# A planned transformer kernel: teaching the planner that GpSimd and VectorE exclude each other at an SBUF port

## The chip, the cores and the metric

One core of a Trainium2 chip. Time is device time in microseconds (us) for one execution of the whole program. Five engines work side by side, each on its own queue of instructions, in that queue's order: TensorE (PE in the profile, its weight loads PEld), ScalarE (ACT), VectorE (DVE), GpSimd (POOL) and SyncE (SP, which issues the DMAs). They meet at semaphores only.

## What is computed

Two layers, each an attention block and an MLP block, on 2,048 tokens of width 512. The weights of both layers are the same. There are 32 heads of width 16, and the MLP is 1,792 wide. Cut to its core, the reference is:

```python
def attention(x):                       # x is normalised
    q, k, v = split(x @ wqkv)           # 32 heads of 16
    p = softmax(q @ k.T * 16 ** -0.5)   # 2048 x 2048 for each head
    return (p @ v) @ wo
def mlp(x):
    return gelu(x @ w1 + b1) @ w2 + b2
for _ in range(2):
    x = x + attention(layernorm(x))
    x = x + mlp(layernorm(x))
```

Data are bfloat16. With heads this narrow the exponentials of the softmax are the bulk of the work: 2 layers x 32 heads x 2048 x 2048 of them.

## The kernel before

**Tiling.** Scores are computed transposed, keys on the 128 partitions and queries along the row. One *cell* is one matmul of TensorE (L1137): 128 keys by 512 columns, that is one bank of PSUM. There are 4,096 cells. A cell then goes one of two ways:
- to ScalarE: L1466 takes the exponential of two or three cells in one instruction (1,024 or 1,536 columns) and writes bfloat16 tiles `pt`. The two slots for this are PSUM banks 0 to 2 and 3 and 4.
- to VectorE, for some rows of keys (`KD`): L1283 (`dfirst`) turns the scores in PSUM into 16-bit integers that are close to the bits of an exponential, into the tile `du` (`dh` for a single one, `kt` where it lies in borrowed space). L1344 and L1346 (`dchain`) then add constants to make three shifted copies. These two work on 16-bit integers from SBUF to SBUF.

The probabilities are multiplied with the values by matmuls of L1527 into PSUM bank 5, 17 rows for each head: 16 of output and one of the row's sum. `norm` finishes a pass: it may add a stored partial sum (L739), transposes into the one buffer `xt` (L741, L743), takes the reciprocal of the sums into `rc` (L746), multiplies by it into `ott` (L754, on GpSimd or on VectorE; two buffers) and transposes into `otn` (L759). From there the output projection `wo` (matmuls of L512, addition to the residual at L785), the layer norm (L581 to L602, its last multiplication `xln` mostly on GpSimd, its power of -0.5 at L588 on GpSimd), and the MLP (`hpair`, `gelu` at L893, `ytile` with the addition at L925) run for 512 tokens at a time, in the shadow of the following tokens' attention. GpSimd also pads the queries of a pass (`qp`, L1085) and scales values for the integer path (`vc`, L1068).

**What sets the order.** No queue's order is written by hand. While the program is built, on the host, `_Sched` runs every part as a thread that yields operations with a price in microseconds, and keeps a clock for each engine. Again and again `run` takes, for each engine, the operations whose inputs are known; among those that could start at once it picks the one of lowest priority number, else the one that is ready first; and of all engines it places the one with the earliest start. The order of placing becomes the engine's queue, and the semaphores that are needed are put in. Prices are fixed; for example:

```python
yield _Op("dve", 0.08 + 0.14 * n, lambda e: e.tensor_scalar(U[:, 1, 0:n, :], U[:, 0, 0:n, :], SHIFT, None, op0=ALU.add),
eng, cost = ("dve", 0.4) if quick else ("pool", 0.72)
```

An operation's output counts as ready at the end of its price plus a small `LATENCY`. The planner also decides during the run: `attach` and `swap` send a cell to VectorE when a bank and a `du` buffer are free in the plan, and `fill` puts dummy matmuls (L1125) into TensorE's planned idle time[...]; `free` chooses their bank. What the chip does differently from the plan can't be made good later: a queue waits at whatever instruction stands first.

Buffers that a plan must not give out twice are *pools*: `("acq", name)` takes the next free one, `("take", ...)` a certain one, `("rel", ...)` gives it back.

**The end.** When the last exponentials are done, ScalarE does the gelu of the last but one group of 256 tokens (two instructions), while the last group (tiles 14 and 15) still needs `norm`, `wo`, its layer norm, and its whole MLP. Tiles 12 and 13 have only their second MLP product left, in pieces of eight matmuls and a last one of twelve.

Of the kernel before, what the change touches and what calls it, by code (L numbers as in the profile page):

```python
# [31 lines left out]
DU = 9  # L32
# [48 lines left out]
class _Prog:  # L81
# [4 lines left out]
    def __init__(self, sems):  # L86
        self.sems = sems
        self.cnt = {k: 0 for k in sems}
        self.prog = {e: [] for e in self.ENGS}
        self.K = {e: {} for e in self.ENGS}  # L90
        self.ev_k = {}
        self.lastw = {}
        self.reads = {}
# [108 lines left out]
        self.done = False  # L202


LATENCY = {"pe": 0.20, "act": 0.10, "dve": 0.10, "pool": 0.15, "sp": 0.1}


class _Sched:
# [5 lines left out]
    def __init__(self, P):  # L214
        self.P = P
        self.clock = {e: 0.0 for e in P.ENGS}
        self.end = {}
        self.pools = {}
        self.tokens = {}
        self.threads = []  # L220
        self.nseq = 0
        self.mode = "F"
        self.ops = []
        self.stream = []
        self.filler, self.free, self.fills = None, None, set()

    def pool(self, name, slots):
        self.pools[name] = list(slots)
# [66 lines left out]
    def _prio(self, op):  # L295
        return op.prio() if callable(op.prio) else op.prio

    def landed(self, keys):
        return max(self.end.get(self.P.lastw[k], 0.0) if k in self.P.lastw else 1e9 for k in keys)

# [11 lines left out]
    def fill(self, start, nxt):  # L312
        while self.filler and self.mode:
# [17 lines left out]
            self.clock["pe"] = now + into + MM + cold  # L331
            self.end[ev] = self.clock["pe"] + LATENCY["pe"]

    def run(self):
        while True:
            moved = True
            while moved:
                moved = False
                for th in list(self.threads):
                    if self._advance(th):  # L340
                        moved = True
            self.threads = [t for t in self.threads if not t.done]
            best = {}
            for th in self.threads:
                if th.op is None:
                    continue
                e = th.op.eng
                rdy = self._ready(th.op)
                if rdy is None:
                    continue  # L350
                best.setdefault(e, []).append((th, rdy))
            if not best:
                if self.threads:
                    raise RuntimeError("stuck: %r" % [(t.prio, t.block) for t in self.threads])
                return
            pick = None
            for e, cand in best.items():
                now = self.clock[e]
                nowc = [c for c in cand if c[1] <= now]
                if nowc:  # L360
                    ch = min(nowc, key=lambda c: (self._prio(c[0].op), c[0].seq))
                else:
                    ch = min(cand, key=lambda c: (c[1], self._prio(c[0].op), c[0].seq))
                start = max(now, ch[1])
                stop = start + self._cost(ch[0].op)
                for c in cand:
                    if c[0].op.slack is not None and c is not ch and c[1] + c[0].op.slack < stop:
                        ch = c
                        start = max(now, ch[1])
                        break  # L370
                if pick is None or start < pick[0]:
                    pick = (start, e, ch[0])
            start, e, th = pick
            op = th.op
            th.op = None
            if op.late is not None:
                op.late(op, start)
            if e == "pe":
                mode = self.mode
                self.fill(start, op)  # L380
                if mode != self.mode:
                    start = max(self.clock["pe"], start - SW * (op.mode != self.mode) + SW * (op.mode != mode))
            ev = self.P.group(e, op.fns, op.reads, op.writes, op.sem, op.by)
            cost = self._cost(op)
            if e == "pe":
                self.mode = op.mode
                self.note(start + cost - op.cost, start + cost, op)
            self.ops.append((e, start, cost, op.writes[0] if op.writes else ""))
            self.clock[e] = start + cost
            self.end[ev] = start + cost + op.tail + LATENCY[e]  # L390

# [110 lines left out]
class _Plan:  # L502
# [215 lines left out]
    def norm(self, l, seg, g, b, part, final):  # L718

        T = self.T  # L720
        pv = self.bank(b)
        key = "B.%d" % b
        qc, q0, w = seg
        if qc == 0:
            pt, pk = T["PART"][l][:, g, :], "PART.%d.%d" % (l, g)
            over = ["V0.%d" % k for k in range(self.NT)] + ["V01"] if l else []
        else:
            pt, pk = T["PART1"][:, g, :], "PART1.%d" % g
            over = ["K0.%d.%d" % (g // 2, c) for c in range(self.NQ)]
        prev = self.before(l, seg)  # L730
        if final and prev:
            yield ("need", ("ofree",) + prev)
        if not final:
            yield _Op("dve", DV, lambda e: e.tensor_copy(pt, pv), reads=[key], writes=[pk] + over)
            yield ("rel", "pv", b)
            return
        xt = T["XT"]
        if part:
            yield _Op("dve", DV, lambda e: e.tensor_tensor(out=pt, in0=pt, in1=pv, op=ALU.add), reads=[key, pk], writes=[pk])  # L739
            yield ("rel", "pv", b)  # L740
            yield _Op("dve", 0.7, lambda e: e.transpose(xt[:, :], pt), reads=[pk], writes=["XT"])  # L741
        else:
            yield _Op("dve", 0.7, lambda e: e.transpose(xt[:, :], pv), reads=[key], writes=["XT"])  # L743
            yield ("rel", "pv", b)
        x3 = xt[:, :].rearrange("p (k c) -> p k c", c=32)
        yield _Op("dve", 0.23, lambda e: e.reciprocal(T["RC"][:, :].rearrange("p (k o) -> p k o", o=1), x3[:, :, 16:17]),  # L746
                  reads=["XT"], writes=["RC"])
        gb, ts = self.heads(seg, g)
        o = gb % 2
        pool = g < 6 and seg[2] == 512  # L750
        nb = w // 32
        for i, t in enumerate(ts):
            o3 = T["OTT"][:, o, 0:w].rearrange("p (k c) -> p k c", c=32)[:, :, 16 * t:16 * t + 16]
            yield _Op(*(("pool", 0.1 + 0.55 * w / 512) if pool else ("dve", 0.1 + 0.31 * w / 512)), lambda e, i=i, o3=o3: e.tensor_tensor(  # L754
                out=o3, in0=x3[:, i * nb:i * nb + nb, 0:16],
                in1=T["RC"][:, i * nb:i * nb + nb, None].to_broadcast([128, nb, 16]), op=ALU.mult),
                reads=["XT", "RC"], writes=["OTT.%d.%d" % (o, t)])
        if ts[-1] == 1:
            yield _Op("dve", 0.05 + 0.65 * w / 512, lambda e: e.transpose(T["OTN"][:, gb, q0:q0 + w], T["OTT"][:, o, 0:w]),  # L759
                      reads=["OTT.%d.0" % o, "OTT.%d.1" % o],  # L760
                      writes=["OTN.%d.%d" % (gb, t % 4) for t in self.tiles(seg)])
            yield ("give", ("otn", l, seg, gb))

    def heads(self, seg, g):
# [325 lines left out]
    def free(self, now, ahead):  # L1090
        P = self.P
        best = (None, 1e9)
        src = self.source()
        for b in (6, 7, 0, 1, 2, 3, 4, 5) if src else ():
            k = "B.%d" % b
            if k in ahead or b in self.hold or k in P.lastw and not P.reads.get(k) and P.lastw[k] not in self.s.fills:
                continue
            t = max([0.0] + [self.s.end.get(ev, 0.0) + FOLD for ev in P.deps(src, [k]) if ev[0] != "pe"])
            if max(t, now) < max(best[1], now):
                best = (b, t)  # L1100
        k = "B.%d" % PVB
        if best[1] > now and self.pvopen and "VC.0.0" in P.lastw and k not in ahead:
            best = (PVB, 0.0)
        return best
# [65 lines left out]
    def take(self, c, free):  # L1170
        self.scored += 1
        self.left[c[0]] -= 1
        if self.left[c[0]] == 0:
            free.append(self.s.tokens[("qp", c[0])])
# [385 lines left out]
    def run(self):  # L1560
        s = self.s
        self.phase = {}
        s.pool("misc", MISC)
        s.pool("dbank", [])
        s.route = self.route
        s.pool("pv", [PVB])
        s.pool("s", range(len(SLOTS)))
# [54 lines left out]
```

The softmax here doesn't subtract the row's maximum and nothing guards it: scores larger than these inputs give would overflow.

## Time and profile before

| | |
|---|---|
| time, median of 3 | 1588.41 us (1587.63 to 1589.98) |
| profiled span | 1587.3 us |
| ScalarE busy | 1547.1 us |
| TensorE busy | 1424.2 us |
| VectorE busy | 1352.0 us |
| GpSimd busy | 200.5 us, in 250 instructions |
| cells to ScalarE / to VectorE | 3,207 / 889 |

A row of the profile's groups reads: line, engine, operation, output and inputs by the program's names, shape, count; then busy time, mean duration of one in ns; then the engine's idle time just before these instructions and what ended most of it. In a timeline each row has its start, its length, the engine, the line and the instruction; where several like ones follow each other they are one row with a count.

### The profile page before, as it was taken

The numbers are of one execution on the slowest core, as the hardware profiler recorded it, in microseconds if no ns is written. First come the engines' busy times: TensorE is split into PE (matmuls) and PEld (weight loads), VectorE is DVE, ScalarE is ACT, GpSimd is POOL, SyncE is SP. The second block draws the span as 40 slices with busy tenths as digits, with TensorE's granted clock in tenths as the row PEclk, the third lists the DMA queues.
The fourth block names the chain that finished last, engine by engine and source line by source line (L and its number), as shares of the span: only waits on it lengthen the run. The fifth ranks groups of instructions, "written<-read, shape, count | busy, mean of one in ns | idle before, by whom it ended". The sixth has DMA issues, their size and how long they took to land.

```text
span 1587.3 us, 42896 instructions
## 1 busy us (share of the span) xinstructions
PE 1424.2 (90%) x18701; PEld 444.6 (28%) x18701; DVE 1352.0 (85%) x2564; ACT 1547.1 (97%) x1393; POOL 200.5 (13%) x250
## 2 busy tenths in 40 slices
PE   8998888899999898988989998888998889898988
PEld 3222222222222222222222222222222222333344
DVE  5689999888898889978788789899878988998984
ACT  7999999999999999999999999999999999999996
POOL 5200012001100201002120020122001000010000
PEclk9999999999999999999999999999999999999999
DMA  5100001241114311143111510001251105312520
GB/s 140 22 2 1 2 14 41 77 132 46 27 45 130 85 41 28 42 140 74 36 28 48 172 44 28 1 2 33 67 167 43 28 15 151 103 36 87 155 82 29
DMA packets 141767, 96.88 MB, mean 61 GB/s; under 512 B 36877, under 2 KB 141582, under 8 KB 141582
## 3 DMA queue, kind: packets, MB, share of 16 engines
q1 hardware_dynamic: 141582, 94.14, 21.2%
q8 instruction: 149, 2.44, 0.6%
q14 instruction: 36, 0.29, 0.1%
HBM read 84.41 MB, written 2.10 MB: 55 GB/s over the span
## 4 chain that ended last, share of the span: by engine, by line
ACT 67%; PE 29%; DVE 2%; POOL 1%; issue 1%; DMA 0%; ACTq 0%; POOLq 0%
ACT pt L1466 60%; PE ps L512 11%; PE ps L1137 9%; PE ps L1527 8%; ACT g L893 3%; ACT v L1466 2%; ACT kt L1466 1%; ACT q L1466 1%; DVE du L1283 1%; ACT L893 1%; ACT L1466 0%; DMA xf<-xln 0%; PE ps L1125 0%; POOL xln L602 0%; POOL rstd L588 0%
## 5 line engine op out<-in xcount | busy, mean ns | idle before, releaser
L1466 ACT ACTIVATE pt<-ps 128x1536 bf16<-128x1536 f32 (+2 forms) x1261 | 1384.2, 1246 | 15.2 <-PE ps L1137 10.3
L1137 PE MATMUL ps<-qp,kt 32*128 32x512 bf16 x4096 | 538.0, 385 | 140.8 <-ACT pt L1466 106.7
L1283 DVE TENSOR_SCALAR du<-ps 128x512 uint16<-128x512 f32 x711 | 479.7, 685 | 97.5 <-PE ps L1137 89.6
L1527 PE MATMUL ps<-pt,v 128*17 128x512 bf16 (+1 forms) x3368 | 433.8, 359 | 2.3 <-ACT pt L1466 0.8
L1527 PE MATMUL ps<-du,vc 128*17 128x512 bf16 (+1 forms) x2394 | 333.8, 358 | 2.7 <-DVE du L1346 1.4
L1137 PEld LDWEIGHTS ps<-qp,kt 32*128 32x128 bf16 x4096 | 140.6, 91 | 685.9 <-ACT pt L1466 304.2
L1346 DVE TENSOR_SCALAR du<-du 128x2048 uint16<-128x2048 uint16 x361 | 246.3, 687 | 2.5
L1085 POOL TENSOR_SCALAR qp<-q,mask 128x512 bf16<-128x512 bf16 (+1 forms) x91 | 66.3, 728 | 1013.8 <-PE ps L1137 1005.1
L512 PE MATMUL ps<-xf,wr 128*32 128x512 bf16 (+1 forms) x2400 | 170.8, 368 | 1.7 <-DMA xf<-xln 1.1
L1527 PE MATMUL ps<-du,v 128*17 128x512 bf16 (+1 forms) x798 | 154.7, 360 | 1.7 <-DVE xt L743 0.9
L1344 DVE TENSOR_SCALAR du<-du 128x1024 uint16<-128x1024 uint16 x361 | 150.5, 428 | 2.0
L1527 PEld LDWEIGHTS ps<-pt,v 128*17 128x17 bf16 x3368 | 111.8, 89 | 113.0 <-issue 72.9
L512 PE MATMUL ps<-wr,g 128*32 128x512 bf16 x1600 | 123.8, 384 | 5.5 <-ACT g L893 5.0
L1527 PEld LDWEIGHTS ps<-du,vc 128*17 128x17 bf16 x2394 | 92.5, 89 | 62.7 <-issue 27.5
L872 DVE TENSOR_SCALAR g<-ps,hb1t 128x512 bf16<-128x512 f32 (+1 forms) x112 | 79.8, 713 | 13.8 <-PE ps L512 12.9
L1527 PE MATMUL ps<-dh,vc 128*17 128x512 bf16 (+1 forms) x321 | 90.6, 358 | 0.0
L1283 DVE TENSOR_SCALAR dh<-ps 128x512 uint16<-128x512 f32 x96 | 65.8, 685 | 11.5 <-PE ps L1137 10.8
L1283 DVE TENSOR_SCALAR kt<-ps 128x512 uint16<-128x512 f32 x82 | 56.1, 684 | 20.7 <-PE ps L1137 19.9
L512 PEld LDWEIGHTS ps<-xf,wr 128*32 128x32 bf16 x2400 | 53.6, 95 | 61.5 <-issue 33.5
L602 POOL TENSOR_SCALAR xln<-x,rstd,nmr 128x512 bf16<-128x512 bf16 x58 | 58.2, 1008 | 33.3 <-DMA xf<-xln 23.2
L754 POOL TENSOR_TENSOR ott<-xt,rc 128x256 bf16<-128x256 f32 x42 | 29.5, 703 | 178.5 <-DVE rc L746 178.5
L1125 PE MATMUL ps<-vc 128*32 128x512 bf16 x476 | 50.9, 395 | 0.1
(93 smaller groups left out, 1185.2 us busy)
## 6 DMA issues: line engine op xcount, KB each, us to landing
wr<-in_B_w_dram SPq DMA_DIRECT2D x256, 256.0 KB, 2.9
wr<-in_A_wqkv_dram SPq DMA_DIRECT2D x24, 256.0 KB, 2.9
wr<-in_A_wo_dram SPq DMA_DIRECT2D x18, 256.0 KB, 2.9
out_dram<-x SPq DMA_DIRECT2D x16, 128.0 KB, 2.7
g<-in_A_wqkv_dram SPq DMA_DIRECT2D x3, 512.0 KB, 5.1
x<-in_A_x_dram SPq DMA_DIRECT2D x3, 512.0 KB, 8.0
q<-in_B_w_dram SPq DMA_DIRECT2D x3, 512.0 KB, 3.9
kt<-in_B_w_dram SPq DMA_DIRECT2D x4, 256.0 KB, 3.3
```

What stands on the lines that cost most here:

```text
L512: return [lambda e, a=a: e.matmul(out[32 * a:32 * a + 32, :], lhsT=lhsT[:, 32 * a:32 * a + 32], rhs=rhs, start=start, stop=stop, tile_posi ...
L602: yield _Op(eng, cost, lambda e: e.tensor_scalar(T["XLN"][:, x, :], T["X"][:, t, :], T["RSTD"][:, t:t + 1], T["NMR"][:, t:t + 1], op0=ALU. ...
L872: yield _Op("dve", 0.21 + n / 966, lambda e, fc=fc, pb=pb: e.tensor_scalar(T["G"][:, fc, q], pb, T["HB1T"][:, fc:fc + 1], None, op0=ALU.ad ...
L893: lambda e, g=g: e.activation(out=g, in_=g, func=ACT.Gelu_apprx_tanh), reads=gk, writes=gk, prio=2)
L1085: yield _Op("pool", 0.1 + 0.6 * w / 512, lambda e, s=s, q=q, i=i, t=t, w=w: e.tensor_scalar(T["QP"][:, s, w * i:w * i + w], q, T["MASK"][: ...
L1125: fns.append(lambda e, o=o, w=w, a=a, m=m: e.matmul(o, lhsT=w, rhs=rhs, start=start, stop=start, tile_position=(0, m * a)))
L1137: return (lambda e: e.matmul(o, lhsT=lhsT, rhs=rhs, start=True, stop=True, tile_position=(32 * a, 0)), ["K%d.%d.%d" % (l, gb, kt // 4), "Q ...
L1283: yield _Op("dve", 0.68, lambda e: e.tensor_scalar(u, self.bank(b), E_SCALE, E_BIAS, op0=ALU.mult, op1=ALU.add), reads=["B.%d" % b], write ...
L1344: yield _Op("dve", 0.08 + 0.14 * n, lambda e: e.tensor_scalar(U[:, 1, 0:n, :], U[:, 0, 0:n, :], SHIFT, None, op0=ALU.add), reads=key[0], w ...
L1346: yield _Op("dve", 0.08 + 0.28 * n, lambda e: e.tensor_scalar(U[:, 2:4, 0:n, :], U[:, 0:2, 0:n, :], 2 * SHIFT, None, op0=ALU.add), reads=k ...
L1466: yield _Op("act", 0.065 + 0.4267 * n, lambda e, src=src, dst=dst: e.activation(out=dst, in_=src, func=ACT.Exp, scale=0.25), reads=["B.%d" ...
L1527: op.fns.append(lambda e, o=o, lhsT=q[0][0][m], rhs=q[0][1][:, n * m:n * m + n], a=a, st=st, sp=sp: e.matmul(o, lhsT=lhsT, rhs=rhs, start= ...
```

## The change

The planner learns of one more resource. GpSimd's instructions (all but the power, whose output is `RSTD`) and those VectorE instructions that work from SBUF to SBUF in the integer path or write `XLN` are called *locking*. For each of the two engines the last few locking operations are kept with the stretch in which they hold the port: from 0.05 us after the planned start to 0.13 us before the planned end (`HOLD`). When a locking operation is looked at, `unlocked` moves its ready time behind such a stretch of the other engine; VectorE is let through while it follows closely on its own last locking operation. So another operation that is ready earlier may be placed first.

Three things go with it. Because operations may now be held back, `norm` takes `xt` and `ott` from pools, and gives them back when their last reader is placed. The start of `norm` waits for `xt` before it adds to or releases its PSUM bank. And `free` no longer offers bank 5 to the filler in its general list.

No instruction's work, no buffer and no price is changed. The diff, cut to its core:

```diff
+HOLD = (0.05, 0.13)
 LATENCY = {"pe": 0.20, "act": 0.10, "dve": 0.10, "pool": 0.15, "sp": 0.1}
...
+        self.locks = {"pool": [], "dve": []}
+        self.fast = (0.0, 0.0)
...
+    def locking(self, op):
+        w = op.writes[0] if op.writes else ""
+        if op.eng == "pool":
+            return not w.startswith("RSTD")
+        return op.eng == "dve" and (w.startswith("XLN") or w.startswith("DU") and w.split(".")[2] != "0")
+
+    def unlocked(self, op, rdy):
+        if op.eng not in self.locks or not self.locking(op):
+            return rdy
+        now = t = max(rdy, self.clock[op.eng])
+        for a, b in self.locks["pool" if op.eng == "dve" else "dve"]:
+            if a <= t < b and not (op.eng == "dve" and a >= self.fast[0] and t < self.fast[1] + 0.02):
+                t = b
+        return t if t > now else rdy
...
-                best.setdefault(e, []).append((th, rdy))
+                best.setdefault(e, []).append((th, self.unlocked(th.op, rdy)))
...
+            if self.locking(op):
+                self.fast = (start, start + cost) if e == "dve" else self.fast
+                self.locks[e] = self.locks[e][-3:] + [(start + HOLD[0], start + cost - HOLD[1])]
...
         xt = T["XT"]
+        gb, ts = self.heads(seg, g)
+        yield ("acq", "xt")
...
-        gb, ts = self.heads(seg, g)
         o = gb % 2
+        if ts[0] == 0:
+            yield ("take", ("ott", o))
...
+        yield ("rel", "xt", 0)
...
+            yield ("rel", "ott", o)
...
-        for b in (6, 7, 0, 1, 2, 3, 4, 5) if src else ():
+        for b in (6, 7, 0, 1, 2, 3, 4) if src else ():
...
+        s.pool("xt", [0])
+        s.pool("ott", [0, 1])
```

## The prediction, made before the changed kernel was run

> **What bounds the kernel now.** I read the page first: engine shares, then the chain that ended last, then the costliest groups.
>
> ```profile
> PE 1424.2 (90%) x18701; PEld 444.6 (28%) x18701; DVE 1352.0 (85%) x2564; ACT 1547.1 (97%) x1393; POOL 200.5 (13%) x250
> ...
> ACT 67%; PE 29%; DVE 2%; POOL 1%; issue 1%; DMA 0%; ACTq 0%; POOLq 0%
> ...
> L1466 ACT ACTIVATE pt<-ps 128x1536 bf16<-128x1536 f32 (+2 forms) x1261 | 1384.2, 1246 | 15.2 <-PE ps L1137 10.3
> ```
>
> ScalarE (ACT) is the bound: 97% busy, two thirds of the chain, nearly all of it the softmax exponentials of L1466. The other engines matter only when they make an exponential late. The 15.2 us of idle time in the row understates that. Two exponentials that don't have to wait overlap at their ends. From the start times in the trace, a 1,024-wide one is followed by the next after 0.904 us and a 1,536-wide one after 1.331 us (medians of those that nothing holds up). The program has 793 of the first, 540 of the second and one of 512. Their real start-to-start times add up to 759.1 + 723.3 us, against 793 x 0.904 + 540 x 1.331 = 1435.6 us. So about 47 us are lost between exponentials, and that is the whole pool from which a better plan can draw. 41.6 us of it lie in some 160 single delays of over 40 ns.
>
> Next, who is late. The waits, longest in total first, show TensorE's score matmuls (L1137) waiting for VectorE to empty a PSUM bank:
>
> ```profile
> PEld ps L1137 <- DVE du L1283: 89.6, 152, 1.6
> DVE du L1283 <- PE ps L1137: 89.6, 180, 3.1
> ```
>
> The second line warns that VectorE also waits for TensorE. By the last wait that ended before the late score, about 19 of the 41.6 us go to VectorE, 12 to the exponentials themselves (a bank that came free late) and 10 to other matmuls ahead in TensorE's queue.
>
> Then the disputed resource. First VectorE, then GpSimd (POOL), in order of time (start, duration, instruction):
>
> ```profile
> 250.96 0.42 DVE L1344 TENSOR_SCALAR du<-du 128x1024 uint16<-128x1024 uint16 x1
> 251.29 0.84 DVE L1346 TENSOR_SCALAR dh<-dh 128x1024 uint16<-128x1024 uint16 x1
> ...
> 253.25 0.42 DVE L1344 TENSOR_SCALAR du<-du 128x1024 uint16<-128x1024 uint16 x1
> 253.71 0.99 DVE L1346 TENSOR_SCALAR du<-du 128x2048 uint16<-128x2048 uint16 x1
> ```
> ```profile
> 249.45 2.40 POOL L602 TENSOR_SCALAR xln<-x,rstd,nmr 128x512 bf16<-128x512 bf16 x2 [3.61 <-DMA xf<-xln]
> 253.22 0.93 POOL L1085 TENSOR_SCALAR qp<-q,mask 128x512 bf16<-128x512 bf16 x1 [1.37 <-PE ps L1137]
> ```
>
> The same 1,024-element addition takes 0.42 us with GpSimd idle and 0.84 us when a GpSimd instruction is under way; the 2,048-element one 0.99 instead of its median 0.683. Over the trace 37 VectorE instructions last over 100 ns longer than their like, 13.3 us together; on GpSimd 61 do, 27.3 us together. VectorE's instructions that read PSUM are not stretched: L1283 has a mean of 685 ns with a GpSimd instruction beside it and without.
>
> **What the Trainium skill says.** "SBUF — State Buffer", section "Who interferes with whom": a VectorE instruction in a two-port mode and a GpSimd instruction exclude each other, whichever came first holding the shared pair for its whole length. "VectorE: DVE Perf Modes", "Why PSUM operands drop a tier" and the tier table, fit with this: only operands that lie in SBUF reach the two-port modes. The trace agrees on both: 0.42 against 0.84 us, and PSUM readers untouched. "TensorE: Matmul & The Clock Gate", "What's actually happening", says that the array falls to half clock after an idle window of about 3.4 us. The trace has four such stretches; in the table by stage the mean granted clock (third figure from the end) is 0.51:
>
> ```profile
> 425.80:432.70 6.90, 5.95 (x32) 1.08 (x32) 4.79 (x12) 5.61 (x6) 1.22 (x1) 0.51 0.00 0
> 814.90:818.40 3.50, 3.50 (x22) 0.61 (x20) 2.60 (x8) 2.97 (x4) 1.50 (x2) 0.51 0.00 0
> 1152.80:1156.30 3.50, 3.50 (x27) 0.68 (x28) 2.78 (x6) 2.73 (x3) 0.00 (x0) 0.51 0.28 92
> 1299.60:1303.10 3.50, 3.25 (x23) 0.73 (x23) 1.26 (x3) 2.69 (x4) 0.00 (x0) 0.51 0.00 0
> ```
>
> ACT's idle gaps in and just after them come to 4.0 us.
>
> **The change, part by part.** It alters no instruction's work, only order and routing, so I counted the two built programs.
>
> Routing: VectorE takes 887 score cells instead of 889, and the exponentials become 803 of 1,024, 534 of 1,536 and one of 512. On ACT that is 10 x 0.904 - 6 x 1.331 = +1.05, say +1.1 us. It adds straight to the bound.
>
> The lock model (`locking`, `unlocked`, the `locks` lists): nothing is removed from an engine; collisions are to be avoided by letting VectorE take a PSUM reader first, or by holding a GpSimd instruction back. Of the 13.3 us that VectorE is held, most is hidden, since it idles 15% of the time and catches up. I take as exposed the late exponentials before which VectorE had not yet idled as long as it had been held: 7.9 us of the 41.6. Low bound: the ACT idle gaps within 6 us of a held VectorE instruction, 3.7 us, since a share of those would be late by chance. High bound: all 19 us put down to VectorE. I take 7.9.
>
> GpSimd's 27.3 us are worth nothing: it is busy 13% of the span and works ahead (1005 us of its idle time is waiting to pad the next queries), and only 0.7 us of VectorE's idle time waits for its L754.
>
> The `xt` and `ott` pools: they keep one normalisation's buffer until its last reader has been placed. Behind a held first instruction stands the release of the PV bank; VectorE's queue is 85% full and waited 13.1 us before L743 in all, with PV matmuls before it. No cost. Bank 5 leaves the filler's list: fills become 552 + 440 matmuls instead of 476 + 468, 12 sets of four more, in TensorE's idle slots. They may save a cold stretch; I leave the 4.0 us out of the central sum.
>
> The end. Here the order of TensorE's queue changes. Before:
>
> ```profile
> 1563.67 1.05 PE L512 MATMUL ps<-wr,otn 128*32 128x512 bf16 x16 [1.33 <-DVE otn L759]
> 1564.53 2.78 PE L512 MATMUL ps<-q,g 128*32 128x512 bf16 x48
> 1567.12 0.62 PE L512 MATMUL ps<-wr,g 128*32 128x512 bf16 x8
> ...
> 1569.62 0.62 PE L613 MATMUL ps<-ident,xln 128*128 128x128 bf16 x8
> ```
> ```profile
> 1560.83 1.28 ACT L893 ACT_TABLE_LOAD   x1
> 1562.12 3.28 ACT L893 ACTIVATE g<-g 128x1792 bf16<-128x1792 bf16 x2
> ```
>
> The last two tiles' output projections (tiles 14, 15) both finish first, by 1564.53. In the changed program 24 matmuls of tile 12's second MLP product stand before tile 14's last eight, and 36 more before tile 15's. Priced by 48 in 2.59 us: the 24 can't start before the first gelu ends, 1562.12 + 1.64 = 1563.8, so 1565.1; tile 14 to 1565.5; 36 more to 1567.5; tile 15 to 1567.9. On VectorE tile 12's addition (0.69) goes first, so tile 15's ends near 1569.1, and both tiles' statistics stand behind it in the queue. Statistics to first rstd took 1.63 us, rstd and its hand-over some 0.65: 1571.3. Tile 13's addition, ahead of nmr in the queue, ends at 1571.45 + 0.69 = 1572.1; from nmr to the transposed tiles took 2.1 us (1568.61 to 1570.69). The last hidden layer's matmuls then start at 1574.2 instead of 1571.69, and what follows is the same. Cost +2.5 us; bounds 1.5 and 3.
>
> Sum: 1588.4 + 1.1 + 2.5 - 7.9 = 1584.1 us.
>
> **Rivals.**
> A, the sum above: 1584.1. For it: the collisions are plainly there and the planner's prices (0.36 and 0.64 us for the two additions) leave them out.
> B, a wash: only the low bound of 3.7 is won, and the two known costs of 3.6 eat it: 1588.3. For it: VectorE's slack hides most holds. Against it: about 19 us of lateness is VectorE's.
> C, slower: the planner now inserts waits where the chip needed none, the delays only move to other places (some 160 of them are shuffled by any new order), and nothing is won net: 1588.4 + 3.6 = 1592.0, more with another cold stretch of about 1 us. For it: the fall in VectorE cells and the worse end are certain, the gain isn't.
> D, a large gain: the plan is truer everywhere. Of VectorE's 19 us of lateness 17 are not in the 7.9; if half of them, some 8 us and with them the cold gaps, go too: 1584.1 - 8 = 1576. Against it: those delays stand far from any GpSimd work.
>
> **How the numbers follow.** A 0.31, D 0.16, B 0.26, C 0.27. The likeliest is A, 1584.1 us. The shuffle of 160 delays of a quarter microsecond each moves any outcome by some 4 us. The range goes from just under D, 1573, to C with two more cold stretches, 1594. Faster by over 0.2% (3.2 us) is A and D, 0.47; within it B, 0.26; slower C, 0.27.
>
> **What would show it.** VectorE's L1344 and L1346 should lose their maxima near 1.07 and 1.11 us and the 13.3 us of held time should halve or better; GpSimd's xln should come down from a mean of 1.008 us towards its undisturbed 0.77. The late time between exponentials should fall from 47 to about 39 us, ACT's busy time stay within 2 us, and the stretch from the last exponential to the end grow from 26.5 to about 29 us. I am wrong if held time falls and the lateness doesn't (B or C), if cold stretches multiply, or if the end isn't longer.

## The result, and the profile after

The changed kernel takes 1598.86 us, the median of four runs (1597.09 to 1601.84), against 1588.66 us before: a ratio of 1.0066 [1.0048, 1.0083]. It is slower by about 10 us. The profiled execution has a span of 1595.3 us, 8.0 us more than the 1587.3 of before. The granted clock of TensorE isn't the main reason: at the same mean clock of 0.993 two executions of the changed kernel took 1598.7 and 1599.0 us, and six of the kernel before had a median of 1588.4.

The page of the changed kernel first: engine shares, the chain that ended last, the largest group.

```profile
PE 1434.0 (90%) x18734; PEld 448.2 (28%) x18734; DVE 1351.3 (85%) x2552; ACT 1548.1 (97%) x1397; POOL 200.6 (13%) x250
...
ACT 70%; PE 27%; DVE 2%; issue 1%; DMA 0%; POOL 0%; SPq 0%; POOLq 0%; ACTq 0%
...
L1492 ACT ACTIVATE pt<-ps 128x1024 bf16<-128x1024 f32 (+1 forms) x1271 | 1392.5, 1260 | 17.5 <-PE ps L1163 10.9
```

ScalarE is still the bound and its busy time has grown by only 1.0 us. Lines have moved by 26 or so: L1466 is now L1492, L1344 and L1346 are L1370 and L1372, and L1137 is L1163.

Now the resource that the planner has learnt of: one line's instructions, with the shortest, median and longest duration in ns, and then two moments of the timeline, GpSimd first and VectorE second.

```profile
L1370 DVE TENSOR_SCALAR du<-du x359: 275/419/1384, 69.0 to 1559.8; 128x1024 uint16<-128x1024 uint16 x176, 128x512 uint16<-128x512 uint16 x4
...
L1372 DVE TENSOR_SCALAR du<-du x359: 383/684/1153, 70.6 to 1560.6; 128x2048 uint16<-128x2048 uint16 x176, 128x1024 uint16<-128x1024 uint16 x4
```
```profile
543.62 2.82 POOL L623 TENSOR_SCALAR xln<-x,rstd,nmr 128x512 bf16<-128x512 bf16 x2 [0.31 <-DVE nmr L612]
...
625.25 0.75 POOL L778 TENSOR_TENSOR ott<-xt,rc 128x256 bf16<-128x256 f32 x1 [2.97 <-DVE nmr L612]
```
```profile
544.02 0.42 DVE L1370 TENSOR_SCALAR du<-du 128x1024 uint16<-128x1024 uint16 x1
544.48 1.07 DVE L1372 TENSOR_SCALAR du<-du 128x2048 uint16<-128x2048 uint16 x1
...
625.44 0.85 DVE L1370 TENSOR_SCALAR du<-du 128x1024 uint16<-128x1024 uint16 x1
```

The collisions are still there. At 544.48 the 2,048-element addition takes 1.07 us beside an `xln`, and at 625.44 the 1,024-element one takes 0.85 us beside an `ott`; undisturbed they take 0.68 and 0.42, the medians above. Counted as in the prediction (VectorE instructions over 100 ns longer than their like), 37 are held for 14.6 us in all; in the kernel before it was 37 for 13.3. GpSimd's `xln` rose from a mean of 1008 to 1033 ns.

Last, the stretch from the last exponential to the end. The table by stage gives start and end, length, then busy time of TensorE (with its count), of its weight loads, of VectorE, ScalarE and GpSimd, the mean granted clock, and two figures on the DMAs. Before, then after:

```profile
1560.80:1587.30 26.50, 22.32 (x524) 14.16 (x512) 8.94 (x22) 11.35 (x19) 1.07 (x2) 1.00 0.14 42
```
```profile
1564.50:1595.30 30.80, 24.84 (x527) 16.51 (x518) 8.94 (x22) 11.46 (x18) 1.06 (x2) 0.94 0.12 36
...
1578.00:1581.50 3.50, 3.50 (x69) 3.18 (x73) 0.00 (x0) 1.42 (x3) 0.00 (x0) 0.51 0.00 0
```

The tail, as I call the stretch from the last exponential to the end, grew from 26.5 to 30.8 us, and 3.5 us of it now run at half clock. Lateness is the time by which ScalarE's start-to-start times exceed the 0.904 and 1.331 us of the prediction. So the 8.0 us of the profiled execution are three terms: +4.3 in the tail; +1.0 in the exponentials themselves (803 x 0.904 + 534 x 1.331, with the one of 512, makes 1437.1 us against 1436.1); and +2.2 in lateness (49.4 against 47.2), with half a microsecond more outside these sums. A second profiled execution of the same program (`after_again` below) has a lateness of 51.5, so that this term is 2 to 4 us. The prediction wanted it to be -7.9.

The tail can be read in order of time. First TensorE after the change, then the one row of the kernel before that is to be set beside it, then VectorE after the change:

```profile
1567.62 1.48 PE L533 MATMUL ps<-q,g 128*32 128x512 bf16 x24 [1.36 <-ACT g L919]
1568.91 0.62 PE L533 MATMUL ps<-wr,otn 128*32 128x512 bf16 x8
1569.34 1.48 PE L533 MATMUL ps<-q,g 128*32 128x512 bf16 x24
1570.63 0.62 PE L533 MATMUL ps<-wr,g 128*32 128x512 bf16 x8
1571.07 0.40 PE L533 MATMUL ps<-b2row,ones 128*32 128x512 bf16 x4
1571.28 0.62 PE L533 MATMUL ps<-wr,otn 128*32 128x512 bf16 x8
1571.71 2.78 PE L533 MATMUL ps<-q,g 128*32 128x512 bf16 x48
1574.30 0.62 PE L533 MATMUL ps<-wr,g 128*32 128x512 bf16 x8
1574.73 0.40 PE L533 MATMUL ps<-b2row,ones 128*32 128x512 bf16 x4
1576.45 0.91 PE L634 MATMUL ps<-ident,xln 128*128 128x128 bf16 x8 [1.31 <-DVE xln L623]
...
1577.98 4.91 PE L533 MATMUL ps<-xf,kt 128*32 128x256 bf16 x112 [0.28 <-DVE xf L642]
```
```profile
1571.69 3.23 PE L512 MATMUL ps<-xf,kt 128*32 128x256 bf16 x112
```
```profile
1571.52 0.69 DVE L951 TENSOR_TENSOR x<-x,ps 128x512 bf16<-128x512 bf16 x1 [1.25 <-PE ps L533]
1572.12 0.68 DVE L811 TENSOR_TENSOR x<-x,ps 128x512 bf16<-128x512 bf16 x1
1572.72 1.28 DVE L602 BATCH_NORM_STATS2 stats<-x 128x6 f32<-128x512 bf16 x2
...
1575.18 0.69 DVE L951 TENSOR_TENSOR x<-x,ps 128x512 bf16<-128x512 bf16 x1 [0.78 <-PE ps L533]
1575.79 0.15 DVE L612 SCALAR_TENSOR_TENSOR nmr<-mv,rstd 128x1 f32<-128x1 f32 x1
```

Tile 12's second MLP product (the first of its matmuls at 1567.62) stands before the projections `wr,otn` of tiles 14 and 15, tile 12's addition (L951 at 1571.52) before tile 15's (L811), and tile 13's before `nmr`. TensorE works from 1567.62 to 1575.13 without a break, but mostly on the products of tiles 12 and 13, while VectorE can only start on tile 15 at 1572.12. After that TensorE waits 1.31 us for the layer norm's `xln`. The last hidden layer (the x112 row) therefore starts at 1577.98, 13.48 us after the last exponential; before it was 1571.69, or 10.89. Its 112 matmuls then take 4.91 us at the low clock instead of 3.23. So of the tail's +4.3 us, 2.6 are order and 1.7 are clock.

The Trainium skill ("TensorE: Matmul & The Clock Gate", "What's actually happening") has half clock after an idle window of about 3.4 us. The 0.51 in the row above agrees with the half clock, but TensorE wasn't idle for so long: in the 3.4 us ahead of the drop it was busy for half of the time, and its longest pause was the 1.31 us. The four stretches in the prediction are no different: TensorE was busy for 44 to 61% of the 3.4 us ahead, with pauses of 1.1 us at most. What sets off the drop is therefore not shown here.

### The profile page after: what moved, and what is told of

Its sections match the earlier page's. It is cut to its first block, busy times and chain, and to the rows that moved or that the text cites. A ratio compares the mean times of both kernels' runs of the same rounds, so it can differ in the third digit from the quotient of the medians.

```text
span 1595.3 us, 42951 instructions
## 1 busy us (share of the span) xinstructions
PE 1434.0 (90%) x18734; PEld 448.2 (28%) x18734; DVE 1351.3 (85%) x2552; ACT 1548.1 (97%) x1397; POOL 200.6 (13%) x250
## 4 chain that ended last, share of the span: by engine, by line
ACT 70%; PE 27%; DVE 2%; issue 1%; DMA 0%; POOL 0%; SPq 0%; POOLq 0%; ACTq 0%
ACT pt L1492 62%; PE ps L533 10%; PE ps L1163 8%; PE ps L1553 8%; ACT g L919 3%; ACT kt L1492 1%; ACT v L1492 1%; ACT q L1492 1%; PE ps L1151 1%; ACT L919 1%; ACT L1492 1%; DVE du L1309 0%; DMA xf<-xln 0%; DVE du L1370 0%; DVE kt L1309 0%
## 5 line engine op out<-in xcount | busy, mean ns | idle before, releaser
L1492 ACT ACTIVATE pt<-ps 128x1024 bf16<-128x1024 f32 (+1 forms) x1271 | 1392.5, 1260 | 17.5 <-PE ps L1163 10.9
L1163 PE MATMUL ps<-qp,kt 32*128 32x512 bf16 x4096 | 537.3, 384 | 138.8 <-ACT pt L1492 103.4
L1553 PE MATMUL ps<-pt,v 128*17 128x512 bf16 (+1 forms) x3403 | 456.3, 359 | 2.0 <-DVE du L1370 0.7
L1163 PEld LDWEIGHTS ps<-qp,kt 32*128 32x128 bf16 x4096 | 141.0, 91 | 683.2 <-ACT pt L1492 306.6
L1372 DVE TENSOR_SCALAR du<-du 128x2048 uint16<-128x2048 uint16 (+1 forms) x359 | 246.6, 691 | 2.3
L1553 PE MATMUL ps<-du,v 128*17 128x512 bf16 (+1 forms) x796 | 151.2, 361 | 1.7 <-DVE du L1309 0.8
L1370 DVE TENSOR_SCALAR du<-du 128x1024 uint16<-128x1024 uint16 (+1 forms) x359 | 150.0, 429 | 2.2
L1553 PEld LDWEIGHTS ps<-pt,v 128*17 128x17 bf16 x3403 | 116.2, 88 | 115.0 <-issue 75.2
L1553 PEld LDWEIGHTS ps<-du,vc 128*17 128x17 bf16 x2388 | 91.6, 89 | 61.8 <-issue 29.1
L898 DVE TENSOR_SCALAR g<-ps,hb1t 128x512 bf16<-128x512 f32 (+1 forms) x112 | 79.9, 713 | 17.6 <-PE ps L533 16.8
L1309 DVE TENSOR_SCALAR kt<-ps 128x512 uint16<-128x512 f32 x82 | 56.3, 686 | 13.3 <-PE ps L1163 12.2
L623 POOL TENSOR_SCALAR xln<-x,rstd,nmr 128x512 bf16<-128x512 bf16 x58 | 59.7, 1033 | 21.7 <-DMA xf<-xln 13.8
L1151 PE MATMUL ps<-vc 128*32 128x512 bf16 x552 | 55.2, 393 | 0.6 <-DVE du L1309 0.4
L778 POOL TENSOR_TENSOR ott<-xt,rc 128x256 bf16<-128x256 f32 x42 | 30.8, 733 | 194.8 <-DVE rc L769 178.8
```

Source lines behind the costliest of these rows:

```text
L623: yield _Op(eng, cost, lambda e: e.tensor_scalar(T["XLN"][:, x, :], T["X"][:, t, :], T["RSTD"][:, t:t + 1], T["NMR"][:, t:t + 1], op0=ALU. ...
L898: yield _Op("dve", 0.21 + n / 966, lambda e, fc=fc, pb=pb: e.tensor_scalar(T["G"][:, fc, q], pb, T["HB1T"][:, fc:fc + 1], None, op0=ALU.ad ...
L1151: fns.append(lambda e, o=o, w=w, a=a, m=m: e.matmul(o, lhsT=w, rhs=rhs, start=start, stop=start, tile_position=(0, m * a)))
L1163: return (lambda e: e.matmul(o, lhsT=lhsT, rhs=rhs, start=True, stop=True, tile_position=(32 * a, 0)), ["K%d.%d.%d" % (l, gb, kt // 4), "Q ...
L1309: yield _Op("dve", 0.68, lambda e: e.tensor_scalar(u, self.bank(b), E_SCALE, E_BIAS, op0=ALU.mult, op1=ALU.add), reads=["B.%d" % b], write ...
L1372: yield _Op("dve", 0.08 + 0.28 * n, lambda e: e.tensor_scalar(U[:, 2:4, 0:n, :], U[:, 0:2, 0:n, :], 2 * SHIFT, None, op0=ALU.add), reads=k ...
```

## The experiments

Three theories stood against each other. *Collision*: held instructions cost time, and the model either fails to remove them or pays for removing them with waits. *End*: the order of the instructions after the last exponential is the loss. *Reshuffle*: any new input to the planner gives another of many plans, their lengths scatter by more than anything the change does, and the kernel before happens to have a short one.

For the third I use the planner's own clock, the end of VectorE's last instruction that it computes on the host while it places the instructions. It is no time of the chip, but it is a property of each kernel that can be set beside the measured time:

| kernel | lock model | planned end (planner's clock) | measured, us | measured - planned | ratio to before |
|---|---|---|---|---|---|
| before | no | 1571.10 | 1588.66 | 17.6 | 1 |
| after | yes | 1579.62 | 1598.86 | 19.2 | 1.0066 [1.0048, 1.0083] |
| `a_end` | yes | 1577.16 | 1597.24 | 20.1 | 1.0046 [1.0030, 1.0062] |
| `a_nolock` | no | 1578.67 | 1596.83 | 18.2 | 1.0051 [1.0033, 1.0069] |
| `j_typ` | no | 1579.07 | 1598.14 | 19.1 | 1.0063 [1.0049, 1.0076] |
| `j_same` | no | 1571.34 | 1588.12 | 16.8 | 0.9996 [0.9986, 1.0006] |
| `a_best` | yes | 1571.10 | 1591.40 | 20.3 | 1.0015 [1.0006, 1.0025] |
| `e_dv` | yes | 1571.42 | 1588.84 | 17.4 | 0.9992 [0.9985, 0.9999] |
| `be_best` | no | 1567.34 | 1584.62 | 17.3 | 0.9969 [0.9960, 0.9979] |

Each ratio is to the kernel before as it ran beside that kernel; its median there lay between 1588.66 and 1589.65 us, so a difference of 1 us in the fifth column means nothing.

**`a_end`: the changed kernel with the order at the end as before.** The second MLP products of tiles 12 and 13 may not be placed before the last two tiles have had their projection added.

```diff
 # in ytile, ahead of ("acq", "misc")
+        if (l, seg) == (NL - 1, self.segs[l][-2]):
+            for u in self.tiles(self.segs[l][-1]):
+                yield ("need", ("xready", u, 2 * l + 1))
```

> The changed kernel, with the second MLP product of tiles 12 and 13 made to wait in the plan for the residual additions of tiles 14 and 15, so that the end stands in the queues as before. Theory 1 (the order of the end is a cost of its own): the stretch from the last exponential to the end falls from 30.8 back to 26.5 us, the half-clock stretch at 1578 us goes with it, and the time falls by 4.3 us to about 1594.5 us. Theory 2 (the end only shows a delay that comes from elsewhere): under 1.5 us of fall.

Measured 1597.24 us, ratio 1.0046 [1.0030, 1.0062]. The table by stage has the tail back:

```profile
1571.10:1597.90 26.80, 22.55 (x524) 14.40 (x514) 8.93 (x22) 11.34 (x18) 1.06 (x2) 1.00 0.13 42
```

26.8 us at full clock against 30.8. The end of the changed plan is thus worth some 4 us in a trace, but the median gained less, 2 to 3 us, which lies between the two theories, and its interval overlaps that of the changed kernel. (The profiled execution was the slowest of six: its lateness was 56.1 us, with 39 us at half clock.) Most of the 10 us lies elsewhere.

**`a_nolock`: the changed kernel without the lock model.** The two pools and the filler's shorter list of banks stay.

```diff
     def locking(self, op):
+        return False
         w = op.writes[0] if op.writes else ""
```

> The changed kernel with no operation called locking, so that only the xt and ott pools and the filler's bank list remain of the change. Theory 1 (the lock model makes the longer plan): within 2 us of before, 1587 to 1591 us. Theory 2 (the pools or the lost bank 5 cost it): 1594 us or more.

Measured 1596.83 us, 1.0051 [1.0033, 1.0069]. With the model switched off the loss is nearly as large. The table by stage, and TensorE in the tail:

```profile
1562.20:1594.60 32.40, 26.56 (x586) 17.13 (x586) 9.20 (x22) 11.34 (x18) 1.23 (x2) 1.00 0.11 35
```
```profile
1571.82 1.91 PE L534 MATMUL ps<-wr,otn 128*32 128x512 bf16 x32
```

But it lies in another place. The tail is 5.9 us longer than before, at full clock, because all 32 projections of tiles 14 and 15 now stand behind the second products of tiles 12 and 13; lateness is 46.9 us, no more than before, and the exponentials themselves account for the other 1.7 us. So this run does not say that the pools cause the loss of the changed kernel. It says that they too give another plan, and that this plan is as long. The shorter list of banks does nothing: put alone into the kernel before, it yields the very plan of before. The pools forbid little, but they change what is placed first somewhere, and what follows changes with it.

**`b_short`: the kernel before, with GpSimd's instructions cut short.** Order, routing and waits are those of before. After their buffers have been filled once, `xln` and `qp` work on 2 columns and `ott` on one head; the rest of these three results is left out.

```diff
-            T["XLN"][:, x, :], T["X"][:, t, :], ...
+            T["XLN"][:, x, 0:m], T["X"][:, t, 0:m], ...      # m = 2
-            q = T["Q"][:, b, 512 * qc + q0:512 * qc + q0 + w]
+            q = T["Q"][:, b, 512 * qc + q0:512 * qc + q0 + m]  # m = 2
-                out=o3, in0=x3[:, i * nb:i * nb + nb, 0:16],
+                out=o3[:, 0:m, :], in0=x3[:, i * nb:i * nb + m, 0:16],  # m = 1
```

> The kernel before, all queues in the same order, with GpSimd's xln, qp and ott instructions cut to a few columns after their buffers have been filled once; the rest of these tiles is left stale, so that part of the layer norm, of the query padding and of the normalisation is left out. VectorE's held time (13.3 us) should be nearly gone. Theory A (7.9 us of ACT's lateness come from holds): 1580 to 1582 us. Theory B (VectorE's slack hides most of them): 1585 us or more.

Measured 1588.58 us, 0.9996 [0.9987, 1.0005]. One line's instructions (shortest, median, longest in ns), and engine shares:

```profile
PE 1428.1 (90%) x18701; PEld 445.8 (28%) x18701; DVE 1343.0 (85%) x2564; ACT 1547.2 (97%) x1393; POOL 126.0 (8%) x250
...
L1471 ACT ACTIVATE pt<-ps 128x1536 bf16<-128x1536 f32 (+2 forms) x1261 | 1384.5, 1250 | 16.2 <-PE ps L1142 11.4
```
```profile
L1351 DVE TENSOR_SCALAR dh<-dh x96: 364/418/434, 86.2 to 1557.1; 128x1024 uint16<-128x1024 uint16 x96
```
```profile
L1346 DVE TENSOR_SCALAR dh<-dh x96: 362/418/848, 85.8 to 1555.7; 128x1024 uint16<-128x1024 uint16 x96
```

The last line is the kernel before: its longest addition of this kind takes 848 ns, here none goes over 434. VectorE's held time falls from 13.3 to 1.9 us (5 instructions), VectorE is busy 9 us less, and the program takes as long as ever: lateness is 48.3 us against 47.2. Of the gain of 7.9 us that the prediction took from here, nothing shows; the interval leaves room for 2.1 us at most, with nearly all of VectorE's held time gone and no price paid in waits. TensorE's score matmuls also wait for VectorE nearly as long as before (89.6 us in the prediction's lines):

```profile
PEld ps L1142 <- DVE du L1288: 87.1, 148, 1.6
```

A held instruction near a late exponential was not the reason that it was late. One thing the run leaves as it was: GpSimd's own instructions are still held, for 23.0 us (27.3 before).

**`b_twice`: the kernel before, with GpSimd's instructions done twice.** Each `xln`, `qp` and `ott` of GpSimd is issued a second time with the same operands; the planner knows nothing of it.

```diff
     def group(self, eng, fns, reads=(), writes=(), sem=None, by=1, again=False):
+        if eng == "pool" and not again and writes[0][:2] in ("QP", "XL", "OT"):
+            self.group(eng, fns, reads, writes, again=True)
```

> The kernel before, all other queues in the same order, with each of GpSimd's xln, qp and ott instructions done twice. Held time on VectorE should go from 13 to 22 us or more. Theory A (0.6 us of time for each us of holding): 1594 us or more. Theory B (hidden by VectorE's slack): 1592 us or less.

Measured 1632.99 us, 1.0276 [1.0252, 1.0299]: on the side of theory A, but far more than the held time can account for. The waits (engine, instruction, what it waited for; total us, times, longest):

```profile
PE ps L514 <- DMA xf<-xln: 23.9, 11, 3.8
...
ACT pt L1468 <- PE ps L1139: 54.0, 61, 4.1
```
```profile
PE ps L512 <- DMA xf<-xln: 1.1, 2, 0.6
```

The second fence is before. VectorE is held for 24.6 us, 11.3 more than before, while lateness grows by 48.7. Some 23 us of that go with normalised tiles that come late: their transfer to `xf` is then late, and TensorE's queue waits 23.9 us at the matmuls that read it, with the score matmuls behind. The trace also has 82 us at half clock instead of 17; what this adds isn't separated. So the run says that GpSimd's work has to be in time, and says little on the port.

**`j_typ`: the kernel before, one price changed by 1.6 ns.** No part of the change is in it. Its plan ends 8.0 us later than that of before, close to the changed kernel's 8.5.

```diff
-        yield _Op("dve", 0.08 + 0.28 * n, lambda e: e.tensor_scalar(U[:, 2:4, 0:n, :], ...
+        yield _Op("dve", 0.0816 + 0.28 * n, lambda e: e.tensor_scalar(U[:, 2:4, 0:n, :], ...
```

> The kernel before, without any part of the change; only the planned price of L1346 is 1.6 ns higher. The planner's own clock then ends 8.0 us later than before (the changed kernel's: 8.5), with the same order of the end as in the changed kernel. Theory S (the change costs what any reshuffle of a lucky plan costs): 1595 to 1600 us. Theory L (it is the lock model's waits that cost): within 3 us of before, 1586 to 1592 us.

Measured 1598.14 us, 1.0063 [1.0049, 1.0076], the same loss as the change. The page's largest group and the tail:

```profile
L1466 ACT ACTIVATE pt<-ps 128x1024 bf16<-128x1024 f32 (+1 forms) x1279 | 1397.7, 1246 | 22.4 <-PE ps L1137 10.1
```
```profile
1569.20:1598.40 29.20, 22.90 (x522) 14.93 (x522) 8.94 (x22) 11.39 (x19) 1.07 (x2) 1.00 0.12 38
```

ScalarE idles 22.4 us ahead of its exponentials instead of 15.2, and the tail is the longer one (29.2), with the order of the changed kernel but at full clock. VectorE is held for 18.6 us; since `b_short` gained nothing from 11.4 us less, I don't put the loss down to that.

**`a_best`: the whole change, `LATENCY` of TensorE 1.2 ns shorter; `j_same`: the kernel before, the same latency 0.8 ns longer.** Both were chosen because their planned end is that of before, though `j_same` has a clearly different plan (899 cells to VectorE instead of 889).

```diff
 # a_best, in the changed kernel
-LATENCY = {"pe": 0.20, ...
+LATENCY = {"pe": 0.1988, ...
 # j_same, in the kernel before
-LATENCY = {"pe": 0.20, ...
+LATENCY = {"pe": 0.2008, ...
```

> The changed kernel with the planner's latency of TensorE 0.1988 instead of 0.20 us. The lock model is on; the planner's own clock ends where that of the kernel before does (1571.10), and the order of the end is as before. Theory S: 1586 to 1591 us. Theory L: 1594 us or more. If a plan that knows of the port is worth something at equal planned length: under 1585 us.

> The kernel before with the planner's latency of TensorE 0.2008 instead of 0.20 us: other queues, but a plan of equal length (1571.34 by the planner's clock against 1571.10), 10 more cells on VectorE. Theory S: 1586 to 1591 us. If equal plans differ on the chip by much more than 2 us, the planner's clock is no yardstick.

Measured 1591.40 us (1.0015 [1.0006, 1.0025]) and 1588.12 us (0.9996 [0.9986, 1.0006]). The change with a luckier plan gives back 8 of its 10 us, with lock model, pools and all; VectorE is held for 16.5 us in it, longer than before. A different plan of the same planned length takes the same time.

**`be_best`: the kernel before with the guard of `a_end` and `LATENCY` of ScalarE 0.1014.** It was picked as a short plan.

```diff
-LATENCY = {"pe": 0.20, "act": 0.10, ...
+LATENCY = {"pe": 0.20, "act": 0.1014, ...
 # and the three lines of a_end
```

> The kernel before without the lock model, with the end's order fixed as in the first run of the study and the planner's latency of ScalarE 0.1014 instead of 0.10 us: the shortest plan of 600 price shifts, 3.8 us shorter by the planner's clock than before. Theory S: 1582 to 1587 us, faster than both kernels. If the planner's clock tells nothing of this size: 1588 us or more.

Measured 1584.62 us, 0.9969 [0.9960, 0.9979]: it beats both kernels.

```profile
L1469 ACT ACTIVATE pt<-ps 128x1024 bf16<-128x1024 f32 (+1 forms) x1266 | 1387.1, 1264 | 8.5 <-PE ps L1140 3.7
```

ScalarE's idle time ahead of the exponentials is 8.5 us instead of 15.2, and lateness 39.7 instead of 47.2. VectorE is held for 16.5 us, longer than before (13.3): the fastest kernel of all has more collisions than the one it beats.

**`a_short`: the changed kernel with GpSimd cut short as in `b_short`; `e_dv`: `a_end` with one more price changed by 0.4 ns.** `e_dv` was again chosen for its planned end. `a_short` asks if the collisions left in the changed kernel cost anything there.

```diff
 # e_dv, in a_end
-DV = 0.69
+DV = 0.6904
```

> The changed kernel, all queues in the same order, with GpSimd's xln, qp and ott instructions cut to a few columns as in the earlier run (parts of the layer norm, the query padding and the normalisation are left out), so that hardly a collision is left. If the change is slow because its collisions got worse (held time 14.6 us): back to about 1590 us. If collisions cost this kernel nothing, as in the kernel before: within 2 us of the changed kernel, 1597 to 1601 us.

> The changed kernel with its end fixed as in the first run of the study, and the price DV 0.6904 instead of 0.69 us: a second plan that knows of the port and is as long as the plan before (1571.42 by the planner's clock). Theory S: 1586 to 1592 us. If plans with the lock model carry a penalty of their own of 2 us, as the first such plan hints (1591.4): 1591 to 1593 us. If they gain: under 1586 us.

`a_short`: 1595.95 us, 1.0040 [1.0027, 1.0054], held time 3.2 us. `e_dv`: 1588.84 us, 0.9992 [0.9985, 0.9999], a lock-model kernel that is as good as before; 8.4 us better than `a_end`, from which it differs by 0.4 ns in one price.

**`after_again`, `a_short_again`: the changed kernel and `a_short` once more, side by side.** The 2.9 us between their medians could have been noise.

> The changed kernel itself, on one chip with the next run, since its earlier time rests on four executions. If collisions cost the changed kernel nothing: its ratio to before and that of the next run overlap and their medians lie within 2 us. If they cost some 3 us there, as the earlier pair hints: 1598 to 1600 us here.

> The changed kernel with GpSimd's three kinds of instruction cut to a few columns (parts of the layer norm, the query padding and the normalisation are left out), as before. Collisions worth nothing: within 2 us of the changed kernel beside it. Worth some 3 us: 1595 to 1596 us against 1598 to 1600 us.

1599.36 us, 1.0066 [1.0054, 1.0078], and 1598.30 us, 1.0051 [1.0038, 1.0064]. The intervals overlap in both pairs. Taken together, the ten executions of the changed kernel have a mean of 1599.6 us and the thirteen of `a_short` one of 1597.1; if the executions of each pair are dealt out to its two kernels at random, so large a difference comes up in about 2 of 100 cases. So a cost of some 2 us for the collisions in the changed kernel is likelier than none, but not certain. Part of any difference is again the clock: the first profile of `a_short` has no half-clock stretch at the end (tail 29.1), the second has one (30.8). The 29.1 is 2.6 us more than before: the order of the end alone.

**The spread of plans.** For the reshuffle theory I let the planner alone run on many kernels whose only difference is one price moved by at most 2 ns, 600 around each kernel:

```
planned end, planner's clock, us        median    10% to 90%          shortest   longest
600 neighbours of the kernel before     1578.25   1572.78..1585.80    1570.42    1591.50
600 neighbours of the changed kernel    1579.66   1575.28..1584.26    1571.09    1598.25
```

The kernel before, at 1571.10, is as short as the best 13 of its 600 neighbours. The changed kernel, at 1579.62, is a median one: 286 of its 600 are as short. Like with like, median with median, the change lengthens the plan by 1.4 us; 7.1 of the planned 8.5 us are a lucky plan lost. This is the planner's clock: of such plans only those of the table were run on the chip, and they were not drawn at random.

**What follows.** In the table, measured minus planned lies between 16.8 and 20.3 us over plans that differ by 12 us. The planned end orders these kernels, up to 2 or 3 us, whether or not the lock model is in. So the loss of 10 us is 8.5 us of a longer plan (planned idle time of ScalarE 17.6 us instead of 12.9, 1.05 of more exponential work, and 2.6 in the tail) and 1.6 us that the chip adds. That is about the size of the half-clock stretch; that it is this stretch isn't shown. A good part of the scatter is the end: in these runs the tail takes one of three lengths, 26 to 27 us with the order of before, 29 with that of the changed kernel (31 with half clock), and 32 in `a_nolock`. The rest is how late the exponentials come, and that isn't the model's mark either: lateness is 56.1 us in `j_typ` without it and 49.1 in `e_dv` with it. The model does not make the plan truer either: kernels with it end 17.4 to 20.3 us behind their plan, kernels without it 16.8 to 19.1.

## Why the prediction was wrong, point by point

**The lock model recovers 7.9 us: this step failed.** It had two halves, and both are wrong. The collisions were not avoided (13.3 us held before, 14.6 after), and avoiding them in the kernel before is worth nothing that could be measured (`b_short`: held time down to 1.9 us, ratio 0.9996 [0.9987, 1.0005]). The exposed share was taken from late exponentials that had a held VectorE instruction before them; that was coincidence in time. The prediction's own figures warned of it: under D it says that of the 19 us whose last wait was for VectorE 17 are not in the 7.9, so that only some 2 of the 7.9 us had VectorE as their last wait. I had written that most of the held time is hidden because VectorE catches up in its idle 15%. That held for all of it, as far as can be measured. Even the low bound of 3.7 us was too high.

Why the model removes no collisions on this chip can be seen by setting actual starts against planned ones. A GpSimd instruction and its VectorE neighbours are off against each other by a standard deviation of 0.46 us before and 0.51 after, more than the mean hold of 0.36 us (13.3 over 37). In the plan, overlaps between the two engines' locking instructions fell from 43.0 to 31.8 us; in the traces they rose from 59.7 to 64.8. The Trainium skill is right that the two exclude each other ("SBUF — State Buffer", "Who interferes with whom"; 0.42 against 0.85 us above), but a plan that misses the moments by half a microsecond can't use it. That this is the reason was worked out from the two traces and not tried by itself.

The prediction also read too little from its lines. It set 0.42 us "with GpSimd idle" against 0.84 and 0.99. But both 0.42 us additions that it shows, at 250.96 and 253.25, have a GpSimd instruction issued beside them, which is the one that waits: the second of the two `xln` takes 1.65 us instead of 0.77, and the `qp` 0.93 instead of 0.69. Where the two meet, either can be the one that is held.

**A shuffle of 160 delays moves any outcome by some 4 us: the assumption that this is centred on zero failed.** It was in the text only to widen the range. By the table and the spread of plans it is the main cause. The kernel before stands at the short end of its neighbours, so that a new order loses 7.1 us in the middle (planner's clock), and `j_typ` showed the loss on the chip with nothing of the change in it: 1.0063 [1.0049, 1.0076]. Rival C had the words for it ("the delays only move") but priced the moving at nothing, and so came to 1592.0, 7 us short.

**The end, +2.5 us: the order was right, the clock was missed.** Counted from the last exponential, the working put `nmr` at the end of 11.3 us and the start of the last hidden layer at 13.4; the trace has 11.29 and 13.48. "What follows is the same" was the error: the 112 matmuls ran at half clock, +1.7 us, in both profiles of the changed kernel. With it the tail grew by 4.3. Without it, as in the first profile of `a_short`, it grows by 2.6, so the +2.5 was right for what it priced.

**Routing, +1.1 us:** right, 1.0 by the same count and in ScalarE's busy time (1547.1 to 1548.1).

**Pools and bank 5 at no cost:** wrong for the pools. They made no wait that I could find, but `a_nolock` shows that they can move the plan by as much as the whole change: 1.0051 [1.0033, 1.0069], most of it in the tail. Bank 5 was right.

**GpSimd's own 27.3 us at nothing:** it stayed at 27.1 us, so the change did not test it. Nor did `b_short`, where 23.0 us of it remain. For it speaks `be_best`, the fastest kernel, where GpSimd is held for 34.7 us. `b_twice` adds that GpSimd's time costs nothing only while its tiles come in time.

**What would show it:** held time did not fall, lateness went up and the end grew. The prediction's sign that it was wrong, "held time falls and the lateness doesn't", was seen in `b_short`, where held time did fall.

**Open:** which decision of the planner first makes the exponentials later, whether the collisions left in the changed kernel cost 0 or up to some 3 us, and what sets off a half-clock stretch.

## What to carry to other kernels

Where a program's order comes from a greedy planner, every edit to it is two edits: what it means to do, and a draw of a new order. Measure the second by itself, with price changes too small to mean anything (here 1.6 ns moved the time by 0.63%), before the first is credited or blamed, and compare medians of such families (done here in the planner's clock alone). A stall that shows in the trace is worth its length only if the end moves when it is taken away, and shortening the instructions that cause it, with the order kept, tells this in one run.

## What the runs showed of the hardware

- VectorE and GpSimd meet not only at semaphores. A VectorE addition of 1,024 elements from SBUF to SBUF takes 0.42 us, or 0.84 to 0.85 when a GpSimd instruction holds it up; at other times it is GpSimd's `xln` that waits and takes 1.65 us instead of 0.77. VectorE's L1283, which reads PSUM, takes 685 ns with GpSimd beside it or not.
- GpSimd's small instructions keep a large part of their time. Undisturbed (medians in `b_short`, then before): `xln` on 2 columns 343 ns against 775 on 512, `qp` 266 against 694, `ott` of one head 216 against 623. Their means, 583, 307 and 276 ns, are longer because VectorE still holds them up. So `b_short` cut GpSimd's busy time only from 200.5 to 126.0 us; yet VectorE was hardly held any more (1.9 us).
- Half-clock stretches are not a property of a program alone: the changed kernel's two profiled executions had 19.3 and 25.9 us of them, the other kernels but `b_twice` 10 to 39, and `b_short` had 30.0 with a time equal to that of before, whose profile had 17.1. Those that don't run past the end of the program last 3.41 or 6.83 us, all of them. In the 3.41 us ahead of one, outside `b_twice`, TensorE was busy for 34 to 70% of the time and paused for 2.2 us at most: it needn't stand idle throughout for its clock to fall.
- One kernel's time follows the mean granted clock. The kernel before took 1594 to 1595 us in its six executions at 0.988 and 1586 to 1587 in its ten at 0.996, about 1 us for each 0.001.
